# Attention and mixture of experts on one core: two requests change places, and one head's values stand later in the order

## The chip, the cores and the metric

The kernel runs on one core of a Trainium2 chip. The core has five engines with a queue of instructions each: TensorE (PE, matrix products; the loads of its stationary operand are shown as PEld), VectorE (DVE), ScalarE (ACT), GpSimd (POOL) and SyncE (SP). Each queue runs in order, and a queue waits for another through semaphores. Transfers between the main memory (HBM) and the on-chip memory (SBUF) run on DMA engines of their own, after GpSimd or SyncE has issued a request. Products are written to eight PSUM banks, from which ScalarE and VectorE read them.

The metric is the device time of one execution in microseconds (us), lower is better. The kernel before has a median of 375.86 us in three runs (375.83 to 376.34).

## The reference

Two stages. First attention over 4 batches, 8 heads, 768 positions and head width 64. Heads 0, 2 and 6 are retrieval heads: they see every earlier position. The other five are streaming heads: they see 4 sink positions and a window of 64. Then a mixture of 4 experts is computed for all 3072 tokens of width 512, with a hidden width of 1024; every expert runs on every token, weighted by its normalised probability.

```python
scores = scale * np.matmul(q, k.transpose(0, 1, 3, 2))
...
scores = np.where(mask[None, :, :, :], scores, -1000000000.0)
scores = scores - np.max(scores, axis=-1, keepdims=True)
a = np.exp(scores)
a = a / (np.sum(a, axis=-1, keepdims=True) + 1e-09)
return np.matmul(a, v).astype(np.float32)
...
p = domain_probs / (domain_probs.sum(-1, keepdims=True) + 1e-09)
for e in range(E):
    h = np.maximum(x @ w1[e], 0.0)
    out += p[:, e:e + 1] * (h @ w2[e])
```

Inputs and output are float32; the kernel computes its products in 16 bits.

## The kernel before

**Groups.** Attention is done in eight groups: batch b and half c of its positions (384 each), numbered g = 2b + c. Group 0 runs alone at the start. From then on the experts' products run on PE, and the steps of the next attention group are woven between them: `moe_steps` yields after each small piece of expert work, and a plan says how much attention should be done by then. Group 1 (batch 0, second half) is woven into the first part of the expert work, which takes three tiles of 128 tokens through one expert after the other (`plain_steps`): layer 1 (L1148, products with `w1sb`, followed by a Relu on ScalarE, L1161), then layer 2 (L1169, products with `w2sb`, added up by VectorE, L1181 and L1185). The order on every engine is the order in which this program calls the instructions.

**Requests.** Weights, and the inputs of group 1, are requested from GpSimd's queue in one list written by hand (lines 562 to 588). `landed(x)` is a tiny copy on GpSimd that waits until x has arrived, so that the list does not run too far ahead. `load_triples` (L230) brings k and q of group 1, `load_v` brings values (L304 for retrieval heads, into `vR`; L310 for streaming heads, into `vS`), `load_w1` (L327) and `load_w2` (L349, L354) bring an expert's weights. `load_w1` makes two requests, one for each half of the partitions; `load_v(0, 1, RH)` makes three, one for each retrieval head. In the built program a request also waits until the eighth request before it has landed.

**One attention group.** `attention(b, c)` first transposes k and q (for group 1 with products on PE, L622, copied to `qT`, `kR` and `kS` by VectorE at L637, L645 and L661; `kR` holds the keys of retrieval heads, `kS` those of streaming heads). Then it goes through the heads in `order`; group 1's is 0, 2, 1, 3, 6, 5, 7, 4. `scores(h)` makes one or more score tiles: products into a bank of `pA` (L736), the exponential on ScalarE into one of eight `es` buffers (L754), the mask on VectorE (L761 or L765). A retrieval head of group 1 has four tiles, a streaming head two. `values(h)` multiplies them with the values: L799 for retrieval heads (15 products of 65 columns in group 1, in several steps, with the normalisation at L824 to L828 and a transposing DMA on SyncE at L833 behind them), L863 for streaming heads (scaled by ScalarE's L878 and L881 and VectorE's L884).

A head's values come later than its scores. The loop holds the heads whose values are due in `waiting` and takes the first one out when two are waiting, or when one is waiting and the score tiles of the waiting heads and the new one are more than six. `both` then alternates steps of the new head's scores with steps of those values:

```python
ahead = sum(len(score_tiles(x)) for x in (*waiting, h))
if len(waiting) > 1 or (waiting and ahead > 6):
    done = waiting.pop(0)
    v_steps = values(done)
for m, step in enumerate(both(scores(h), v_steps)):
```

For groups 0 and 1 (`by_dma` false) the transposes of k and q stand between the heads; those of heads 6 and 7 (`transposes(3)`) come inside head 2's scores.

Of the kernel before, what the change touches and what calls it, by code (L numbers as in the profile page):

```python
# [19 lines left out]
def kernel(  # L20
# [36 lines left out]
    E, DM, F = moe_w1.shape  # L57
# [110 lines left out]
    def half(u):  # L168
        return slice(u * D, (u + 1) * D)
# [5 lines left out]
    def own_v(h):  # L175
        return half(PLACE[h][1])
# [10 lines left out]
    def v_tiles(b, c, h):  # L187

        if RETR[h]:
            return vR[b % 2][:, 3 * c : 3 * c + 3, RH.index(h), :]  # L190
        if b:
            return windows(vSf)[:, :, SH.index(h), :]
        return vS[:, c, :, SH.index(h), :]
# [10 lines left out]
    def rows_of(x, b, h, c):  # L204
        return x[b, h, c * CH : (c + 1) * CH, :].rearrange("(j p) d -> p j d", p=P)

    def tiles_of(x, b, h, c):
        return x[b, h, c * CH : (c + 1) * CH, :].rearrange("(t r) d -> r t d", r=TK)

    def windows_of(x, b, h, c):  # L210

        assert b > 0
        first = ((b * H + h) * S + c * CH - WO) * D
        return bass.AP(x.tensor, x.offset + first, [[D, P], [WQ * D, WT], [1, D]])
# [13 lines left out]
    def load_triples(x, dst, b, c, h0, h1):  # L228

        gp.dma_start(  # L230
            out=dst[:, h0:h1, :, :].rearrange("p h j d -> p h (j d)"),
            in_=x[b, h0:h1, c * CH : (c + 1) * CH, :].rearrange(
                "h (p j) d -> p h (j d)", j=3
            ),
        )
# [64 lines left out]
    def load_v(b, c, heads):  # L300
        for h in heads:
            t = v_tiles(b, c, h)
            if RETR[h]:
                gp.dma_start(out=t[:, :, 0:D], in_=rows_of(v, b, h, c))  # L304
            elif b:
                gp.dma_start(  # L306
                    out=t[:, :, own_v(h)], in_=windows_of(v, b, h, c)
                )
            else:
                gp.dma_start(  # L310
                    out=t[R0:P, :, own_v(h)],
                    in_=tiles_of(v, b, h, c),
                )
# [10 lines left out]
    def load_w1(e, f0, f1):  # L324
        x = moe_w1[e].rearrange("(u c d) f -> u d c f", u=2, c=DMP)
        for u in range(2):
            gp.dma_start(  # L327
                out=w1sb[half(u), e * DMP : (e + 1) * DMP, f0:f1],
                in_=x[u, :, :, f0:f1],
            )  # L330
# [219 lines left out]
    def landed(x):  # L550

        gp.tensor_copy(out=seen, in_=x)
# [5 lines left out]
    def w2_of(e):  # L558
        return w2sb[0:1, e * FTP, 0:1]
# [17 lines left out]
    landed(qt16[0:1, 0, 0, 0:1])  # L577
    load_triples(k, k16, 0, 1, HP, H)
    load_triples(q, qt16, 0, 1, HP, H)
    load_v(0, 1, RH)  # L580
    load_w1(2, 0, F)
    landed(w2_of(1))
    load_v(0, 1, SH[:2])
    load_w2(2)
# [15 lines left out]
    def attention(b, c):  # L600
# [238 lines left out]
        def x_transposes(h):  # L839
            ct = PLACE[h][0]  # L840
            x = x_pair if ct else x_one
            r = slice(0, P) if ct else half(0)
            ps = pV.tile([P, 512], FP32, name="pV", bufs=2)
            for j in range(3):
                nc.tensor.matmul(
                    out=ps[r, j * P : (j + 1) * P], lhsT=x[:, j, r], rhs=ident16,
                    start=True, stop=True,
                )
            nc.vector.tensor_copy(out=xT[g][r, ct, :], in_=ps[r, 0:CH])

        def values(h):
            if RETR[h]:
                yield from values_r(h)
                return
            ct, u = PLACE[h]
            ps = pV.tile([P, 512], FP32, name="pV", bufs=2)
            work = []
            for es, parts in es_of[h]:
                for t, o, q0, nq in parts:
                    work.append((es, t, o, q0, nq))  # L860
            ns = 0
            for n, (es, t, o, q0, nq) in enumerate(work):
                nc.tensor.matmul(  # L863
                    out=ps[:, q0 : q0 + nq],
                    lhsT=v_tile(b, c, h, t),
                    rhs=es[:, o : o + nq],
                    start=(n == 0),
                    stop=(n == len(work) - 1),
                    skip_group_check=True,
                )  # L870
                ns += mm_ns(nq)
                if ns > 300 and n < len(work) - 1:
                    yield ns
                    ns = 0

            r, o = half(u), half(1 - u)
            rc = att.tile([P, CH], FP32, name="rc", bufs=2)
            nc.scalar.activation(  # L878
                out=rc[r, :], in_=ps[o, 0:CH], func=AF.Ln, bias=eps[o, :]
            )  # L880
            nc.scalar.activation(out=rc[r, :], in_=rc[r, :], func=AF.Exp, scale=-1.0)  # L881

            def scale(r=r, ps=ps):
                nc.vector.tensor_tensor(  # L884
                    out=xT[g][r, ct, :], in0=ps[r, 0:CH], in1=rc[r, :], op=ALU.mult
                )

            later(scale, g)

            yield ns + (600.0 if g == 1 else 400.0)  # L890
# [36 lines left out]
        def both(a, bb):  # L927

            gens = [a, bb]
            while gens:  # L930
                for gg in list(gens):
                    try:
                        yield next(gg)
                    except StopIteration:
                        gens.remove(gg)

        by_dma = b > 0
        if not by_dma:
            alloc_qT(b, c)
        if first:  # L940
            yield from transposes(0)
            yield from scores(0)
            yield from scores(1)
            yield from transposes(2)
            yield from values(0)
            yield from scores(4)
            yield from scores(5)
            x_transposes(0)
            yield from transposes(1)
            yield from values_pair(1, 5)  # L950
            yield from scores(3)
            yield from transposes(3)
            yield from scores(2)
            yield from values(4)
            yield from both(scores(6), values(2))
            yield from scores(7)
            yield from values(6)
            yield from values_pair(3, 7)
            x_transposes(6)
            tick(LAG)  # L960
            small_things()
        else:
            order = (0, 2, 6, 1, 3, 5, 7, 4) if by_dma else (0, 2, 1, 3, 6, 5, 7, 4)
            more = divmod(g + 1, NCH) if g + 1 < G else None
            if not by_dma:
                sink_rows(b, c)

            def behind_values(h):
                if more and not RETR[h]:
                    load_v(*more, [h])  # L970
            if by_dma:
                keys_to_rows(b, c)
                yield 1500.0
            else:
                yield from transposes(0)
                yield from transposes(1)

            waiting = []
            for n, h in enumerate(order):
                v_steps, done = iter(()), None  # L980
                ahead = sum(len(score_tiles(x)) for x in (*waiting, h))
                if len(waiting) > 1 or (waiting and ahead > 6):
                    done = waiting.pop(0)
                    v_steps = values(done)
                for m, step in enumerate(both(scores(h), v_steps)):
                    yield step
                    if not by_dma and n == 1 and m == 1:
                        yield from transposes(3)
                if done is not None:
                    behind_values(done)  # L990
                waiting.append(h)
                if n < 3 and by_dma:
                    keys_to_windows(b, c, n)
                if n == 1 and by_dma:
                    sink_rows(b, c)
                if n == 3 and more and g > 1:
                    transpose_rows(*more)
                if not by_dma and n == 2:
                    yield from transposes(2)
            if more:  # L1000
                if g == 1:
                    load_probs(pair0)
                    transpose_rows(*more)
            for h in waiting:
                yield from values(h)
                behind_values(h)
# [39 lines left out]
    def tick(ns):  # L1046
        clock[0] += ns
        while behind and behind[0][0] <= clock[0]:
            behind.pop(0)[1]()
# [561 lines left out]
    for ns in attention(0, 0):  # L1611
        tick(ns)
# [108 lines left out]
```

## Time and profile before

| | |
|---|---|
| median of three runs | 375.86 us (375.83 to 376.34) |
| the profiled execution's own time | 376.48 us |
| its span, first to last instruction | 374.8 us |
| granted TensorE clock | 0.999 |
| GpSimd's requests in the stretch: L304 x3, L327 x2 | 34.37 to 36.59, 36.59 to 37.85 |
| first matmul of the third expert's layer 1 | 46.92 |
| `landed` on GpSimd behind those weights | 46.91, after 4.06 us of waiting |

The table of line groups shows what the expert work and the attention cost on each engine, with columns: line, engine, operation, output and inputs, shape, count, busy time, mean of one in ns, idle time before them and what ended it.

```profile
L1148 PE MATMUL pA<-xT,w1sb 128*128 128x384 f16 (+1 forms) x256 | 30.4, 272 | 1.9 <-DMA w1sb<-in_moe_w_dram 1.8
L1169 PE MATMUL pO<-w2sb,hA 128*128 128x512 f16 x128 | 30.6, 379 | 0.0
L736 PE MATMUL pA<-qT,kR 128*128 128x128 f16 (+2 forms) x141 | 23.1, 261 | 0.7 <-DVE kR L645 0.7
```

Busy time of PE is modelled up to the end of a matmul, while the next one already streams; the distance from start to start is the better measure of what one costs.

### The profile page before, as it was taken

Reading aid. Unit: us, or ns where it says so; the run is one execution under the profiler, and the core shown is the slowest. Engines: PE = TensorE matmul, PEld = TensorE weight load, DVE = VectorE, ACT = ScalarE, POOL = GpSimd, SP = SyncE. Lnnn points to the kernel's source line nnn. Section 1 sums busy time; section 2 is a strip of 40 time slices with the busy share of each in tenths; the row PEclk is TensorE's granted clock in tenths of the full one; section 3 lists DMA queues with packets and bytes.
Section 4 is the critical chain, followed back from the end, with each engine's and each line's share of the span. In section 5 each row is a group of like instructions: output and inputs, shape, how many; then the busy total and the mean of one; then the engine's idle time right before and its main releaser. Section 6 shows DMA issues by size and latency. Waiting matters only on the chain.

```text
span 374.8 us, 10310 instructions
## 1 busy us (share of the span) xinstructions
PE 365.4 (98%) x4219; PEld 310.5 (83%) x4219; DVE 277.9 (74%) x583; ACT 226.3 (60%) x471; POOL 113.0 (30%) x162
## 2 busy tenths in 40 slices
PE   7899899999999999999999999999999999999996
PEld 4655466678998988999989899988899998998995
DVE  4765867797787669868657858857768868979881
ACT  5644569547786785775776855784777361451630
POOL 8845573692057039015501650320000000000000
PEclk9999999999999999999999999999999999999999
DMA  9999999999799399988905990951220300300101
GB/s 181 190 208 207 196 172 191 182 205 106 111 104 160 83 98 129 158 109 76 189 3 65 172 153 13 140 121 12 72 68 2 108 10 2 114 3 14 44 3 58
DMA packets 122340, 39.65 MB, mean 106 GB/s; under 512 B 112192, under 2 KB 114820, under 8 KB 122292
## 3 DMA queue, kind: packets, MB, share of 16 engines
q0 software_dynamic: 82816, 19.01, 57.1%
q1 hardware_dynamic: 37876, 19.58, 23.5%
q8 instruction: 33, 0.54, 0.6%
q10 hardware_dynamic: 1600, 0.39, 0.5%
q14 instruction: 15, 0.12, 0.1%
HBM read 44.89 MB, written 6.34 MB: 137 GB/s over the span
## 4 chain that ended last, share of the span: by engine, by line
PE 85%; DMA 8%; POOL 4%; DVE 1%; issue 1%; ACT 0%; POOLq 0%
PE pO L1462 31%; PE pA L1282 22%; PE pO L1311 9%; DMA w1sb<-in_moe_w_dram 5%; PE pA L1148 5%; PE pA L736 5%; PE pO L1169 5%; DMA q<-in_q_dram 3%; PE pV L1311 2%; PE pA L1311 2%; PE pV L863 2%; PE pV L799 2%; DVE xs L1233 1%; POOL vR L304 1%; PE pA L1554 0%
## 5 line engine op out<-in xcount | busy, mean ns | idle before, releaser
L1462 PEld LDWEIGHTS <-hA 128*128 128x128 f16 x1104 | 104.8, 98 | 11.9
L1282 PE MATMUL pA<-xs,w1sb 128*128 128x256 f16 x768 | 97.2, 272 | 0.0
L1282 PEld LDWEIGHTS <-w1sb 128*128 128x128 f16 x768 | 71.8, 98 | 7.3
L1462 PE MATMUL pO<-w2sb,hA 128*128 128x256 f16 x640 | 76.8, 272 | 0.0
L754 ACT ACTIVATE es<-pA 128x384 f16<-128x384 f32 (+2 forms) x122 | 58.9, 511 | 27.5 <-PE pA L736 22.9
L1291 ACT ACTIVATE hA<-pA 128x512 f16<-128x512 f32 x96 | 57.2, 598 | 29.1 <-PE pA L1282 26.8
L306 POOL DMA_DIRECT2D vS<-in_v_dram x30 | 29.6, 988 | 113.2 <-PE pV L863 109.9
L1462 PE MATMUL pO<-tsb,hA 128*128 128x256 f16 x464 | 56.8, 272 | 0.0
L1233 DVE TENSOR_TENSOR xs<-xT,pB 128x1024 f16<-128x1024 f16 (+1 forms) x49 | 47.0, 976 | 2.7 <-DMA xT<-x_pair 2.7
L1067 DVE TENSOR_TENSOR hA<-hA 128x1024 f16<-128x1024 f16 x60 | 39.4, 684 | 0.6 <-PE pO L1462 0.3
L1161 ACT ACTIVATE hA<-pA 128x384 f16<-128x384 f32 (+1 forms) x64 | 22.2, 385 | 20.4 <-PE pA L1148 20.4
L1311 PEld LDWEIGHTS <-w1sb 128*128 128x128 f16 x512 | 31.3, 98 | 1.6 <-issue 0.5
L1148 PE MATMUL pA<-xT,w1sb 128*128 128x384 f16 (+1 forms) x256 | 30.4, 272 | 1.9 <-DMA w1sb<-in_moe_w_dram 1.8
L1169 PE MATMUL pO<-w2sb,hA 128*128 128x512 f16 x128 | 30.6, 379 | 0.0
L1148 PEld LDWEIGHTS <-w1sb 128*128 128x128 f16 x256 | 19.5, 98 | 10.9 <-issue 2.5
L1482 ACT COPY s<-pO 128x256 f32<-128x256 f32 x31 | 11.5, 372 | 27.3 <-PE pO L1462 21.8
L765 DVE TENSOR_TENSOR es<-es,mS 128x384 f16<-128x384 f16 (+1 forms) x40 | 13.8, 344 | 17.9 <-ACT es L754 17.9
L884 DVE TENSOR_TENSOR xT<-pV,rc 64x384 f16<-64x384 f32 x36 | 20.0, 555 | 8.3 <-ACT rc L881 7.7
L1328 DVE CUSTOM_DVE_ANT_0 hA<-pO,s 128x512 f16<-128x512 f32 x26 | 17.7, 688 | 9.9 <-PE pO L1311 8.5
L878 ACT ACTIVATE rc<-pV,eps 64x384 f32<-64x384 f32 x36 | 20.7, 576 | 6.6 <-PE pV L863 6.0
L1321 ACT COPY s<-pO 128x512 f32<-128x512 f32 x39 | 22.7, 587 | 3.2 <-PE pO L1311 3.0
L736 PE MATMUL pA<-qT,kR 128*128 128x128 f16 (+2 forms) x141 | 23.1, 261 | 0.7 <-DVE kR L645 0.7
(175 smaller groups left out, 519.1 us busy)
## 6 DMA issues: line engine op xcount, KB each, us to landing
pB<-p_rows SPq DMA_DIRECT2D x10, 512.0 KB
out_dram<-o SPq DMA_DIRECT2D x19, 256.0 KB
w1sb<-in_moe_w_dram POOLq DMA_DIRECT2D x8, 512.0 KB, 9.2
w2sb<-in_moe_w_dram POOLq DMA_DIRECT2D x4, 1024.0 KB, 12.1
vS<-in_v_dram POOLq DMA_DIRECT2D x30, 112.0 KB, 4.4
k_rows<-in_k_dram POOLq DMA_DIRECT2D x18, 128.0 KB, 5.3
q<-in_q_dram POOLq DMA_DIRECT2D x18, 128.0 KB, 6.2
out_dram<-hA SPq DMA_DIRECT2D x4, 256.0 KB
```

The source lines that it names most:

```text
L306: gp.dma_start(out=t[:, :, own_v(h)], in_=windows_of(v, b, h, c))
L736: nc.tensor.matmul(out=ps[:, o : o + nq], lhsT=key_tile(b, c, h, t), rhs=qTs[b, c][:, hp, q0 : q0 + nq], start=(n == 0 or not first), stop ...
L754: nc.scalar.activation(out=es[:, 0:cols], in_=ps[:, 0:cols], func=AF.Exp, scale=SC)
L1067: nc.vector.tensor_tensor(out=out, in0=a, in1=b, op=ALU.subtract)
L1148: nc.tensor.matmul(out=pss[ft][:, 0:cols_n], lhsT=w1_tile(e, ct, ft), rhs=x[:, ct, :], start=(n == 0), stop=(n == DMP - 1),)
L1169: nc.tensor.matmul(out=ps_o, lhsT=hs[:, ft, j * P : (j + 1) * P], rhs=w2sb[:, e * FTP + ft, :], start=(ft == 0), stop=(ft == FTP - 1),)
L1233: nc.vector.tensor_tensor(out=o, in0=xin, in1=pb.to_broadcast([P, DMP, n, P]), op=ALU.mult)
L1282: nc.tensor.matmul(out=ps[:, f * PC : (f + 1) * PC], lhsT=w1_tile(e, ct, f0 + f), rhs=xs[:, ct, :], start=(ct == 0), stop=(ct == DMP - 1),)
L1291: nc.scalar.activation(out=blocks[:, b0 : b0 + 2, k0 : k0 + 2, :].rearrange("p t f x -> p f t x"), in_=ps.rearrange("p (f t x) -> p f t x" ...
L1311: nc.tensor.matmul(out=ps[:, f * P : (f + 1) * P], lhsT=w_tile(e, w[:, ct, :], f), rhs=a[:, ct, :], start=(first and f == 0 and ct == 0), ...
L1321: nc.scalar.copy(out=kept[n], in_=ps)
L1462: nc.tensor.matmul(out=ps, lhsT=a[:, k, :], rhs=b(k), start=(first and k == 0), stop=(k == KT - 1), skip_group_check=not first,)
```

## The change

Two edits. In the list of requests, the three requests of group 1's retrieval values go behind the two of the third expert's first weights. In `attention`, the bound of six score tiles becomes eight for the groups 0 and 1, of which only group 1 uses this loop. In group 1 heads 0 and 2 have eight tiles together, which is more than six and not more than eight; so head 0's values are no longer taken out at head 2 but at the next head, 1, when two heads are waiting.

```diff
     load_triples(q, qt16, 0, 1, HP, H)
+    load_w1(2, 0, F)
     load_v(0, 1, RH)
-    load_w1(2, 0, F)
     landed(w2_of(1))
...
                 ahead = sum(len(score_tiles(x)) for x in (*waiting, h))
-                if len(waiting) > 1 or (waiting and ahead > 6):
+                if len(waiting) > 1 or (waiting and ahead > (6 if by_dma else 8)):
                     done = waiting.pop(0)
```

In the built program the same instructions stand on every engine in both versions. On PE, head 2's four score tiles come without head 0's values between them; the first seven of head 0's 15 values products then follow head 1's first score tile and precede the third expert's first layer-1 products, and the other eight stand around that expert's next tile. On VectorE the normalisation of head 0 (L824 to L828) goes behind the two masks of head 1. On GpSimd only the two requests change places. From the transposes of heads 4 and 5 (`transposes(2)`) on nothing is moved.

## The prediction

> **What bounds the kernel now.** The page's busy table comes first: TensorE (PE) is busy 98% of the span, so a change can only win where PE stands still, and only loses where it makes PE stand still.
>
> ```profile
> span 374.8 us, 10310 instructions
> PE 365.4 (98%) x4219; PEld 310.5 (83%) x4219; DVE 277.9 (74%) x583; ACT 226.3 (60%) x471; POOL 113.0 (30%) x162
> ```
>
> Next the chain of waits between 34 and 50 us, where the diff acts. Columns: start, length, what held the end.
>
> ```profile
> 34.37 2.22 POOL vR L304 x3
> 36.59 0.62 POOL w1sb L327
> 37.21 9.58 DMA w1sb<-in_moe_w_dram
> 46.79 0.14 issue
> 46.92 0.81 PE pA L1148 x4
> ```
>
> The third expert's first weights (two requests, L327) stand behind three requests of group 1's retrieval values (L304) on GpSimd, and the second half lands at 46.79. The reader is to see that PE starts that expert (L1148) only then. After 46.92 this chain holds PE work almost alone up to 110 us, so what PE gains or loses here reaches the end. Third, PE's timeline before that start:
>
> ```profile
> 41.66 0.27 PE L799 MATMUL pV<-vR,es 128*128 128x65 f16 x3 [0.18 <-ACT es L754]
> 45.59 0.33 PE L736 MATMUL pA<-qT,kR 128*128 128x384 f16 x1
> 46.92 0.81 PE L1148 MATMUL pA<-xT,w1sb 128*128 128x384 f16 x4 [1.01 <-DMA w1sb<-in_moe_w_dram]
> ```
>
> Two stops: one for an exponential, one of 1.01 us for the weights. The listed busy time hides part of them, since ends of matmuls are modelled; by starts, a 384-column matmul takes 0.163 (24 of L1148 from 49.14 to 53.05), so PE was free at 45.59 + 0.17 = 45.76 and stood 1.16. At 41.19 four L799 matmuls began, which take 0.12 at 0.03 each (seven from 45.13 to 45.34); the next began at 41.66, another 0.35. Together 1.5 us, the most that this place can give. Fourth, VectorE's timeline, which decides my forecast:
>
> ```profile
> 42.51 0.36 DVE L761 TENSOR_TENSOR es<-es,mC 128x384 f16<-128x384 f16 x1 [1.68 <-ACT es L754]
> 42.78 0.68 DVE L1067 TENSOR_TENSOR tsb<-w2sb,tsb 128x1024 f16<-128x1024 f16 x1
> 43.38 0.74 DVE L1185 SCALAR_TENSOR_TENSOR hA<-pO,p_sb,hA 128x512 f32<-128x512 f32 x1
> 44.05 0.79 DVE L637 CAST qT<-pA 128x384 f16<-128x384 f32 x1
> 44.68 0.80 DVE L645 CAST kR<-pA 64x384 f16<-64x384 f32 x1
> 45.49 0.81 DVE L661 CAST kS<-pA 64x384 f16<-64x384 f32 x1
> ```
>
> From 42.51 these six run without a gap, and the last, which writes head 7's keys into kS, ends at 45.49 + 0.81 = 46.30.
>
> **Part one, the requests.** Nothing is added: three L304 requests (0.74 each, 2.23) and two L327 (0.62 each, 1.26) change places. The weights are requested at 34.37 instead of 36.59, the values at 35.63 instead of 34.37. What this does to landing is read from the DMA view of single issues (last column: us from issue to landing):
>
> ```profile
> q<-in_q_dram POOLq DMA_DIRECT2D x1, 192.0 KB, 6.0
> vR<-in_v_dram POOLq DMA_DIRECT2D x1, 48.0 KB, 5.7
> w1sb<-in_moe_w_dram POOLq DMA_DIRECT2D x1, 512.0 KB, 7.3
> ```
>
> The request ahead of all five, q at 33.63, lands at 39.63; the third vR (35.8) at 41.5; the first half of w1 (36.59) at 43.9, the second at 46.79. They land in the order of issue, one behind the other, with the DMA engines busy throughout. So the values occupy 41.5 − 39.63 = 1.9 us, and without them in front the weights land at about 44.9. The bounds: no gain, if they were only interleaved (46.79), and 2.2, the whole shift of the issue (44.6). I take 1.9. The first vR took 0.85 behind q (34.37 + 6.1 = 40.5), hence lands at about 45.75.
>
> What GpSimd issues behind them keeps its order. In the built program each request waits for the landing of the eighth before it, so the last three vS requests (40.84 to 42.85) now wait for the two halves of w1 and the first vR, up to 45.8. They stand behind the third expert's w2 in the queue, which lands at 52.45 (39.95 + 12.5) either way, and head 5, their first user, comes past 60. The fourth expert's w1 (47.38) goes out some 0.5 earlier at best, behind the same transfers; it landed at 60.0 for a use at 61.52. This costs nothing; if that cover were gone, L1148 at 61.52 would be late next.
>
> **Part two, the order on PE.** The test `ahead > 6` becomes 8 for group 1 only. Head 0's values (15 L799 matmuls in group 1) no longer run between head 2's scores but between those of head 1. The same instructions remain, 15 matmuls of about 0.03 each moved past the first L1148. PE after the change, from 41.19 (start of what follows head 2's first scores, the same in both): two 256-column scores 0.22 (44.05 to 44.27 before), four L1169 0.86 (44.27 to 45.13), twelve L622 0.45 (42.72 to 43.17), four L1169 0.86, two scores 0.22 (45.34 to 45.56), four L1169 0.86, one 0.17: 44.83. None of these meets a wait; the exponentials whose banks they take end by 43.0.
>
> Now comes head 1's first score tile, ahead of head 0's values and L1148. **Its second weight load waits in the built order for the L661 copy that ends at 46.30.** Before, the same wait stood behind L1148 (47.57), where it cost nothing. That copy doesn't move: it is the end of the gapless row that starts when ScalarE has done head 2's first exponential (42.48), which stays fifth in ScalarE's order; the exponential that is newly early comes behind it. So the wait on weights turns into a wait on VectorE, from 44.83 to 46.30. Then: release 0.08 (an estimate between the 0.02 and 0.14 that "issue" takes in the chain), two score matmuls 0.11 (three take 47.57 to 47.74), seven L799 0.21: L1148 starts at 46.70 instead of 46.92, with weights (44.9) and vR (45.75) there. What is left to do differs: eight L799 more (0.25), one score tile less (0.17). Net 0.22 − 0.08 = **0.14 us gained** of the 1.5.
>
> ScalarE's exponential for head 1 takes a buffer that head 0's fourth values matmul frees (46.8 on); the Relu of L1148 behind it is ready at 47.5, so nothing is held. VectorE's normalisation of head 0 (L824 to L828, 0.15 + 0.18 + 0.36) slides behind head 1's masks, as does SP's transposing DMA (48.50, then about 49.5); its result is next touched by L884 at 57.55. The PSUM bank of L637 (49.61 + 0.80 before) is free for the third hidden tile of those 24 L1148 at about 50.3 against a need at 50.3; a hundredth or two may be lost.
>
> **Sum.** 376.48 (the profiled run's own time, 374.8 of it span, 1.7 around it) − 0.14 = 376.34. The median shown is 0.62 lower, 375.86; the same step gives **375.7**.
>
> **Rivals.** (1) *The copy does not hold PE.* If VectorE is through earlier than this execution shows, vR's landing decides: values at 45.75, L1148 at 45.96, gain 0.96 − 0.08 = 0.88: 375.0. For it: part one truly clears the weights. Against: the wait is in the built order and the six VectorE rows have no gap to lose.
>
> (2) *Slower: the copy pins PE where the weights did not.* The profiled run is 0.62 longer than the median; if the DMA wait is part of that, PE waits less for w1 in ordinary runs, while the copy holds the new order all the same. Without any wait the old order starts L1148 at 45.76, the new one at 46.70 with 0.08 more to do: 1.02 lost, 376.9. It decides as soon as w1 lands before some 46.65 in the old order, and passes 0.75 lost at about 45.9. Against: L661 itself hangs on earlier PE work, and q and k loads came through the same queue.
>
> (3) *The values come late.* vR now stands behind 1 MB of weights, and PE's in-order queue holds L1148 behind the values. The two vS requests that followed w1 before landed 8.8 and 8.5 us after issue (46.9, 47.3); at 47.3 L1148 starts at 47.5 and 0.7 is lost: 376.5. It decides from a landing past 46.5. Against: the bytes in front are the same as those that had landed by 46.79. Issues of 0.62 for w1 at 36.59, during L637 and L645 (36.78 to 38.2), are as long as all others (617 to 637 ns), so GpSimd does not look locked out. The Trainium skill (SBUF — State Buffer, "SBUF: two separate sides") warns of that lockout: VectorE in a two-port mode keeps GpSimd from writing descriptors. By that rule vR, now issued during the same copies, would be what suffers; the row speaks against it.
>
> (4) *The weights land no sooner.* w1 still at 46.79: L1148 at 46.92, 0.08 lost, 375.9; within the forecast's own range.
>
> **Chances.** Forecast with (4) 0.56; (1) 0.24; (2) 0.13; (3) 0.07. A difference under 0.2% (0.75 us) is about what a measurement of this kernel can tell from no change. (1) ends faster in nearly all its share, 0.23 in total. (2) and (3) pass 0.75 in the greater part: slower 0.16. The rest, 0.61, is within. The range reaches to (1) and to most of (2): 374.9 to 376.7; the forecast's own is 375.4 to 376.1.
>
> **What would show it.** Right: no wait on w1sb at the first L1148 of that expert, a PE stop of about 1.5 us charged to VectorE at the kS scores (L736) ending near 46.4, vR landing after w1 by 46. Wrong: a stop charged to vR, L661 ending before 45.5, or a w1 wait that stays; and a difference past 0.75 either way.

## The result: slower by a quarter of a per cent

The changed kernel has a median of 376.93 us (14 runs, 375.89 to 378.59), the kernel before on the same chip 375.98 (14 runs, 375.58 to 377.24). The ratio is 1.0025, with an interval of 1.0013 to 1.0037. Two later series of the same program gave 1.0015 (1.0007 to 1.0024) and 1.0019 (1.0006 to 1.0032). So the loss is real, 0.6 to 0.95 us by the medians of the three, where 0.14 us of gain had been forecast; 376.93 also lies above the range, which ended at 376.7.

The first trace of the changed kernel (time 376.67 us, the one of before had 376.48) does not look like a failed forecast. From the page of its profile, the same lines as before:

```profile
span 374.9 us, 10308 instructions
...
PE 364.9 (97%) x4219; PEld 310.2 (83%) x4219; DVE 278.1 (74%) x583; ACT 226.5 (60%) x471; POOL 113.7 (30%) x162
...
L1148 PE MATMUL pA<-xT,w1sb 128*128 128x384 f16 (+1 forms) x256 | 30.4, 273 | 1.3 <-DMA w1sb<-in_moe_w_dram 1.2
```

The idle time of L1148 for `w1sb` fell from 1.8 to 1.2 us, and all that is left of it belongs to the first expert, at 20.8 us. In PE's timeline the third expert no longer waits for weights:

```profile
45.12 0.26 PE L736 MATMUL pA<-qT,kS 128*128 128x64 f16 x2
46.52 0.24 PE L736 MATMUL pA<-qT,kS 128*128 128x160 f16 x1 [1.14 <-DVE kS L661]
46.60 0.38 PE L799 MATMUL pV<-vR,es 128*128 128x65 f16 x7
46.82 0.81 PE L1148 MATMUL pA<-xT,w1sb 128*128 128x384 f16 x4
```

The wait stands where it had been foreseen, at head 1's scores, on VectorE's copy into `kS`. The chain of waits (start, length, what held the end) shows what is behind it: VectorE's row without a gap, from the moment ScalarE had done head 2's first exponential.

```profile
41.19 1.48 ACT es L754 x3
...
42.69 0.36 DVE es L761
43.05 0.60 DVE tsb L1067
43.65 0.66 DVE hA L1185
44.31 0.71 DVE qT L637
45.02 0.63 DVE kR L645
...
45.66 0.81 DVE kS L661
46.48 0.05 issue
46.52 0.24 PE pA L736
```

The requests did what they should. The two halves of the third expert's first weights were issued at 34.55 and 35.17 and landed at 42.06 and 44.68, the three values right behind them, at 44.89, 45.21 and 45.54. The DMA view of the issues from 33.5 to 36.5 us, whose last column is the time from issue to landing (the median of both halves in the first line, the first value in the second):

```profile
w1sb<-in_moe_w_dram POOLq DMA_DIRECT2D x2, 512.0 KB, 8.5
...
vR<-in_v_dram POOLq DMA_DIRECT2D x1, 48.0 KB, 9.1
```

From the first expert's first product (20.79; before 20.55) to the run of 24 products of the third (49.02; before 49.14) this execution took 28.23 us, against 28.59 before. By this pair of traces the change wins 0.36 us in its stretch, and loses 0.27 near 247 us, where PE waits for VectorE and that for a transposing DMA (x_pair, L833). Neither explains a loss of 0.6 to 0.95.

### The profile page after: what moved, and what is told of

Its sections match the earlier page's. It is cut to its first block, busy times and chain, and to the rows that moved or that the text cites. A ratio compares the mean times of both kernels' runs of the same rounds, so it can differ in the third digit from the quotient of the medians.

```text
span 374.9 us, 10308 instructions
## 1 busy us (share of the span) xinstructions
PE 364.9 (97%) x4219; PEld 310.2 (83%) x4219; DVE 278.1 (74%) x583; ACT 226.5 (60%) x471; POOL 113.7 (30%) x162
## 3 DMA queue, kind: packets, MB, share of 16 engines
HBM read 44.89 MB, written 6.34 MB: 137 GB/s over the span
## 4 chain that ended last, share of the span: by engine, by line
PE 85%; DVE 6%; DMA 5%; POOL 1%; issue 1%; ACT 1%; POOLq 0%; DVEq 0%
PE pO L1462 29%; PE pA L1282 21%; PE pO L1311 9%; PE pA L1148 7%; PE pO L1169 7%; PE pA L736 4%; DMA w1sb<-in_moe_w_dram 2%; PE pV L1311 2%; PE pA L1311 2%; PE pV L799 2%; DVE xs L1233 2%; PE pV L863 2%; DMA xT<-x_pair 1%; DMA hA<-in_v_dram 1%; DVE hA L1067 1%
## 5 line engine op out<-in xcount | busy, mean ns | idle before, releaser
L1148 PE MATMUL pA<-xT,w1sb 128*128 128x384 f16 (+1 forms) x256 | 30.4, 273 | 1.3 <-DMA w1sb<-in_moe_w_dram 1.2
L1148 PEld LDWEIGHTS <-w1sb 128*128 128x128 f16 x256 | 19.4, 98 | 10.1 <-issue 1.7
```

Of the source, the lines that this page charges most:

```text
L1148: nc.tensor.matmul(out=pss[ft][:, 0:cols_n], lhsT=w1_tile(e, ct, ft), rhs=x[:, ct, :], start=(n == 0), stop=(n == DMP - 1),)
```

## The experiments

Four explanations were tried. P: the steps are right and the rest is chance. C: a long stop of PE lets the clock fall in part of the executions. D: a transfer is late elsewhere, through the new order of the requests. R, the second rival of the prediction: in ordinary executions of before the weights come sooner than in the one trace of it, so that the copy holds PE where the weights did not. S is the opposite of R: the long wait of the first trace is the usual one. All ratios are to the kernel before in the same series.

**The changed program again (e1, e9, and single traced executions e15, e17, e18).** Only a comment was added.

> The changed kernel once more, nothing edited. Theory P (the step as predicted, the rest is chance between executions): ratio to the kernel before between 0.998 and 1.001. Theory C (the new long stop of PE, 1.1 to 1.4 us on the key copy, makes the clock gate drop in part of the executions): ratio 1.002 to 1.004, and where an execution is long its granted clock is near 0.995. Theory D (a transfer moved by the new order of requests is late in part of the executions): ratio 1.002 to 1.004 at a clock of 1.000.

> The changed kernel with a comment added. Two things decide: its ratio, and what TensorE waits for. Theory R (the copy holds TensorE until 46.5 us in every execution of the changed kernel, where in before the weights let it go at 45.9 in some executions and at 46.9 in others): the stop on kS L661 of 1.0 to 1.2 us is there again, first product of the third expert near 46.8, ratio 1.001 to 1.0025. Theory D (a transposing transfer near 245 us comes late in the changed kernel more often): a wait of 0.2 us or more at the product near 247 us.

> The changed kernel, one more look. Theory R: TensorE stands for 1.0 to 1.2 us on VectorE's copy into kS, as in all three traces of it, however early the weights land; theory S the same. They differ in before alone; this look counts the two kernels evenly.

> The changed kernel, a look to count with. Theory R: the stop on VectorE's copy into kS again 1.0 to 1.2 us, the 24th product of the third expert starting 0.1 to 0.4 us sooner after the first expert's first product than in the first trace of before (where it took 28.6 us); the other looks at before have 0.3 to 0.8 us sooner. What is lost apart from that (start at 20 us, product at 247 us) lies between -0.5 and 0.5 us.

> A second look of the same kind. Theory R: a stop of 1.0 to 1.2 us on VectorE's copy into kS, and the 24th product of the third expert 0.1 to 0.4 us sooner after the first expert's first product than in the first trace of before.

Measured: e1 376.65 us (11 runs), e9 376.72 (11 runs), with the ratios given above; the single executions took 375.96, 376.00 and 376.50. The stop on `kS` was 1.1 us in each of these traces. P falls, since three series agree on a loss.

**The kernel before again (e5, and single traced executions e6, e13, e14).** Here, too, only a comment was added.

> The program of before with a comment added. Its median should be the one of before (ratio 1.000, interval within 0.15% either way); any larger difference is what two builds of one program show here. Its trace: theory S (the stop of 1.5 us for the third expert's weights in the first trace is usual) expects TensorE to wait 1.0 to 1.3 us for w1sb(2) again, with w1(2) landing 26.0 to 26.5 us after the first expert's first product. Theory R (the second rival of the prediction: in ordinary executions the weights come sooner than in the trace of before, so that the copy pins TensorE where the weights did not) expects a wait of 0.8 us or less. Theory C (the stop at 20 us for the first expert's weights can be followed by a stretch at half the clock) expects none here if that stop is under 1 us.

> Before again, one look. The same three expectations as for the other look at before: S a wait of 1.0 to 1.3 us for w1sb(2), R 0.8 us or less; C a full clock from the first stretch on. The time should lie in 375.4 to 377.5.

> Before, one more look at how long TensorE waits for w1sb(2). Theory R: the landing of these weights wanders by a microsecond between executions of before (46.79, 46.77 and 45.76 us in three), and the wait with it (1.0, 0.8 and none); a fourth should again lie between none and 1.1, and the stretch from the first expert's first product to 49 us be shorter the shorter the wait is. Theory S: 1.0 or more, 45.76 was an exception.

> The same question as the look before it: theory R a wait between none and 1.1 us, theory S 1.0 us or more.

Measured: e5 376.13 us (12 runs; ratio 0.999, 0.9969 to 1.001); the single executions 376.27, 375.99 and 375.99. What matters is PE's timeline of e5 around the third expert's start:

```profile
45.65 0.33 PE L736 MATMUL pA<-qT,kR 128*128 128x384 f16 x1
45.90 0.81 PE L1148 MATMUL pA<-xT,w1sb 128*128 128x384 f16 x4
...
48.11 1.46 PE L1148 MATMUL pA<-xT,w1sb 128*128 128x384 f16 x8
49.77 1.46 PE L1148 MATMUL pA<-xT,w1sb 128*128 128x384 f16 x8 [0.20 <-DVE qT L637]
```

The expert starts at 45.90 instead of 46.92, and no wait for weights is listed, since they had landed at 45.76. At 49.77 a small wait appears that the first trace did not have: VectorE's copy of queries (L637), which frees a PSUM bank. Of the 1.02 us that came free, this takes back 0.35. All traces of the two kernels together (times in us; "PE at 60" and "at the end" compare the start of the same matmul with the first trace of before; + is later):

| execution | weights landed | first expert's first L1148 | run of 24 L1148 | PE at 60 | at the end | time |
|---|---|---|---|---|---|---|
| before, first | 46.79 | 20.55 | 49.14 | 0 | 0 | 376.48 |
| before, e5 | 45.76 | 20.67 | 48.11 | -0.68 | -0.71 | 375.77 |
| before, e6 | 46.77 | 20.80 | 49.12 | -0.02 | -0.21 | 376.27 |
| before, e13 | 46.00 | 20.74 | 48.35 | -0.61 | -0.52 | 375.99 |
| before, e14 | 46.20 | 20.26 | 48.55 | -0.60 | -0.49 | 375.99 |
| changed, first | 44.68 | 20.79 | 49.02 | -0.12 | +0.15 | 376.67 |
| changed, e1 | 45.14 | 20.85 | 49.30 | +0.16 | -0.04 | 376.45 |
| changed, e9 | 44.63 | 20.60 | 48.84 | -0.31 | -0.13 | 376.38 |
| changed, e15 | 45.45 | 20.45 | 48.81 | -0.34 | -0.53 | 375.96 |
| changed, e17 | 44.81 | 20.58 | 48.81 | -0.33 | -0.52 | 376.00 |
| changed, e18 | 44.83 | 20.62 | 48.86 | -0.28 | -0.01 | 376.50 |

In before the landing wanders by a microsecond and PE's start with it; the first trace had the latest landing of the five. Counted from start to start, as the prediction counted its 1.16 us, PE stood 1.16, 0.08, 0.95, 0.23 and 0.91 us for these weights, in the order of the table. (In e14 they landed early, but the whole execution ran 0.3 us ahead.) In the changed kernel the weights land 0.8 us apart and it makes no difference, because the copy sets the start: from the first expert's first product to the run of 24 it takes 28.23 to 28.45 us, the kernel before 27.44 to 28.59, the less the shorter that stop.

The means at 60 us are -0.38 for before and -0.20 for the changed kernel, so on average it is 0.18 us behind there, and 0.21 at the end. S falls: the first trace had the longest stop, and two of five have next to none. The means have the sign that R expects, but executions of before alone differ by 0.7, so that with five and six traces the standard error of the 0.18 is about 0.17; the sign is not settled by them. The times of these profiled executions differ in the mean by 0.23 (376.10 and 376.33), the medians of the timed series by 0.6 to 0.95.

**Only the requests (e2).** Before, with the weights requested ahead of the values, and PE's order as it was:

```diff
-    load_v(0, 1, RH)
     load_w1(2, 0, F)
+    load_v(0, 1, RH)
```

> Only the requests change places; head 0's values stay between head 2's scores. All theories expect PE to stop at the first L799 of head 0 from about 41.3 until the first vR lands, 44.9 in the changed kernel's trace: 3.6 us, against 1.5 us of stops that go. Ratio 1.005 to 1.007 by the sum. If the clock gate reacts to a long stop (theory C), 3.4 us or more of half clock come on top: 1.009 and more, and clocks near 0.995. Theory D expects long executions here at full clock, as the requests are those of the changed kernel.

Measured: 381.15 us (4 runs), ratio 1.014 (1.0122 to 1.0157), far above the 1.005 to 1.007 of the sum. PE's list of waits from 15 to 60 us (total, times, longest):

```profile
PE pV L799 <- DMA vR<-in_v_dram: 3.0, 1, 3.0
PE pA L1148 <- DMA w1sb<-in_moe_w_dram: 2.1, 1, 2.1
```

Head 0's values, in their old place, wait 3.0 us for `vR`. So the first edit needs the second and can't be priced by itself. The rest of the 5 us is, in this trace, the second line (the first expert's weights, 0.8 before) and a stretch at half the clock from 21.2 us on, both ahead of the place where the edit acts. The other three runs have a mean clock of 0.990 to 0.995 too; whether the stop at 46.7 has a part in that is not shown.

**Only the order (e3).** Before, with the bound of eight tiles:

```diff
-                if len(waiting) > 1 or (waiting and ahead > 6):
+                if len(waiting) > 1 or (waiting and ahead > (6 if by_dma else 8)):
```

> Only head 0's values move behind head 2's scores; the requests stay as before, so the weights land near 46.8 and vR near 41. PE stops once, from 44.8 to 46.9. By the sum L1148 starts where it did before with 0.08 us more to do: ratio 1.000 (theory P). Theory C: this stop is the longest of all orders but that of the requests alone, so 1.002 to 1.005, with clocks near 0.995 in the long executions. Theory D: the requests are those of before, so 0.999 to 1.001 and no long executions beyond those of the kernel before.

Measured: 377.00 us (12 runs), ratio 1.0018 (1.0003 to 1.0034). The copy holds PE for 1.1 us here too. The traced execution is one of the two longest (378.56 us), with half the clock from 21.2 to 24.6; the section on the chip shows it. Without its two runs at a mean clock of 0.995 the median is 376.62. Theory P had expected a ratio of 1.000. The order alone is thus enough for a loss like that of both edits (1.0015 in the same series). Whether the earlier weights are worth anything beside it is left open by this run, since the two ratios can't be told apart.

**The copy sooner (e4) and later (e10).** The changed kernel, with head 7's keys copied ahead of head 6's, and with that copy made twice:

```diff
-                for u in range(2):
+                for u in (1, 0) if hp == 3 and not first else (0, 1):
```

```diff
-                    nc.vector.tensor_copy(out=x_out, in_=x_in)
+                    for _ in range(2 if hp == 3 and not first else 1): nc.vector.tensor_copy(out=x_out, in_=x_in)
```

> The changed kernel, and in the transposes of heads 6 and 7 head 7's key copy (L661) runs before head 6's (L645). The stop of PE ends with L661, now at about 45.5 instead of 46.3, 0.8 us sooner. The step of the prediction: L1148 at 46.0, a gain of 0.14 + 0.8 = 0.9 us on the kernel before, ratio 0.9975 (theory P). Theory C: the stop shrinks to 0.3 to 0.7 us and the clock holds: 0.9975 too, with clocks of 1.000. Theory D: the requests are those of the changed kernel, so long executions at full clock remain: ratio 0.999 to 1.001.

> The changed kernel with head 7's copy into kS made twice in group 1 (the second writes the same), so that VectorE lets TensorE go one copy, 0.8 us, later. Theory R, and the prediction's step that the copy is what holds TensorE: the stop grows from 1.1 to 1.9 us and the kernel by 0.7 to 0.8 us: ratio of before 1.003 to 1.0045. If the copy did not set the end, nothing is added: ratio 1.001 to 1.0025. Theory C (a stop of nearly 2 us makes half-clock stretches likelier): some runs at a mean clock of 0.995 with 2 us more.

Measured: e4 376.24 us (12 runs), ratio 0.9999 (0.999 to 1.0009); e10 376.97 us (6 runs), ratio 1.0044 (1.0018 to 1.007), where the changed kernel in the same series had 1.0019. PE's waits of e4 (from 40 to 250 us), then of e10 (from 40 to 60):

```profile
PE pO L1311 <- ACT hA L1291: 0.7, 1, 0.7
PE pA L736 <- DVE kS L661: 0.5, 1, 0.5
```

```profile
PE pA L736 <- DVE kS L661: 2.0, 1, 2.0
```

The stop is 0.5, 1.1 and 2.0 us with the copy 0.8 sooner, in its place, and one copy (0.80) later. PE at 60 us stands at -0.27, -0.20 (the mean of six) and +0.64. The lower end is flatter, partly because this execution of e4 began the first expert late (20.86). So the copy sets the end of this stretch: doubled, it adds 0.84 us there. In the timed runs the ratio of e4 is 0.0016 under that of the changed kernel in the same series, which is 0.6 us, as much as its stop lost; P and C had expected 0.9975, and the number that D had named fits as well. Of e10 the timed runs say less: the median of e10 is 0.25 above that of e9, and its ratio rests in part on one execution of 380.44 at a mean clock of 0.995. The interval is wide enough to hold both the 0.7 to 0.8 expected and no addition at all; it is the trace that decides here. The first line of e4 is the place near 247 us, where that execution lost 0.65.

**No wait in either order (e7, e8).** e7 is before, with the third expert's first weights in halves, so that its first products need half of them; e8 is the changed kernel, with head 7's keys copied by ScalarE, and first (with e4's edit):

```diff
-    load_w1(2, 0, F)
+    load_w1(2, 0, F // 2); load_w1(2, F // 2, F)
```

```diff
-                    nc.vector.tensor_copy(out=x_out, in_=x_in)
+                    (nc.scalar.copy if hp == 3 and not first else nc.vector.tensor_copy)(out=x_out, in_=x_in)
```

> Before, with the third expert's first weights requested as two halves of the columns in the place where they stand, and nothing else: the first products of that expert need the first half alone, which by the trace of before would land near 44 us instead of 46.8. No copy is moved ahead of them, so nothing takes the wait's place but vR's half microsecond at most. Theory S: the 1.16 us of that wait go and nothing comes instead: 375.0 against 376.1, ratio 0.997 (0.996 to 0.998). Theory R: the wait is shorter in ordinary executions, so 0.3 to 0.5 us: ratio 0.9985 to 0.9995. A theory by which the time saved here is eaten by a later wait (the transposing transfer near 245 us): no change, ratio 1.000, with TensorE waiting 0.5 us or more there.

> The changed kernel, but head 7's keys are copied by ScalarE and first, so that TensorE no longer waits for VectorE's copy near 46 us; in the changed kernel that stop is 1.1 us. The prediction's steps (the whole stop of 1.5 us goes when neither copy nor weights hold TensorE, up to vR's landing at 44.9 to 45.9): 374.9 to 375.3, ratio 0.997 to 0.998 of before and 1.3 to 2 us under the changed kernel. Theory R: the same gain against the changed kernel in the step, but from an ordinary before whose stop is shorter: ratio 0.998 to 0.9995. Theory D (the new order of requests costs elsewhere, whatever TensorE does at 46 us): ratio 0.999 to 1.001.

Measured: e7 376.39 us (12 runs), ratio 1.0005 (0.9986 to 1.0025): no gain, where S and R had both expected one; nor does its trace list the wait near 245 us that the third theory named. e8 375.66 us (12 runs), ratio 0.9983 (0.9964 to 1.0002). In e7 the wait for the first weights is gone, the expert starts at 46.05, and by 48.26 PE is 0.88 us ahead of the first trace of before. Then two things take it back: L637 holds PE for 0.28 at 50.0, and the chain of waits shows the second weights:

```profile
41.57 11.67 DMA w2sb<-in_moe_w_dram
53.24 0.04 issue
53.28 1.02 PE pO L1169 x4
```

At 60 us only 0.16 of the 0.88 is left. Without its wait on the first weights, this version is held by VectorE and then by the second weights. The last is in part the edit's own: the second weights were requested at 41.57, behind two requests more, 1.6 us later than in the first trace of before. In e8 both the copy and its share of VectorE's row are away from PE; PE stands at -1.46 at the run of 24, and after a wait for the second weights at -0.88 at 60 us. What is left of waits from 40 us on:

```profile
PE pO L1311 <- DVE xs L1067: 0.5, 1, 0.5
PE pO L1169 <- DMA w2sb<-in_moe_w_dram: 0.4, 1, 0.4
PE pO L1311 <- ACT hA L1361: 0.2, 1, 0.2
```

**The place near 247 us (e11, e12).** e11 is the changed kernel, with the row transposes of the next group issued one head later, so that the transposing DMA of x_pair goes ahead of six others on SyncE. e12 is e8 with that, and with the second weights requested ahead of two values:

```diff
-                if n == 3 and more and g > 1:
+                if n == 4 and more and g > 1:
```

> The changed kernel with the row transposes of the next group's keys and queries issued one head later (n == 4 in place of n == 3), so that the transposing transfer of x_pair goes ahead of six others on SyncE's queue, in every group behind the second. If theory D holds, the wait near 247 us goes (0.3 us in the trace of the changed kernel, none in the one of its second submission) and with it most of what the change costs: ratio 0.9995 to 1.001. Theory R: 0 to 0.3 us less than the changed kernel: ratio 1.0005 to 1.002.

> A candidate to beat both kernels: the changed kernel with head 7's keys copied by ScalarE and first, the transposing transfer of x_pair ahead of the six others, and the third expert's second weights requested before the values of heads 1 and 3. With the first edit alone the trace had 0.4 us of wait for w2sb at 52.5 and 0.5 us at 247 us left; both should go. Expected 0.6 to 0.9 us under that one: ratio of before 0.996 to 0.998.

Measured: e11 379.63 us (6 runs), ratio 1.0105 (1.0085 to 1.0126); e12 378.30 us (5 runs), ratio 1.006 (1.0048 to 1.0072). Both miss by far. PE's waits of e11 from 60 us on:

```profile
PE pA L736 <- DMA qT<-q: 2.3, 2, 1.5
PE pO L1311 <- DVE xs L1067: 0.5, 1, 0.5
```

The six transposes have no slack themselves: one head later, scores wait for `qT` in two places, 1.5 and 0.8 us, and the wait near 247 stays; in e12 it is 0.8 us, and two waits for `qT` cost 0.9. In the 20 traces PE waits between nothing and 0.8 us at that place, as a rule longer where the first transposing issue of `kT` on SyncE is longer (1.85 to 2.64 us in the 18 traces without the edit of e11). The rule is loose: an issue of 2.36 comes with a wait of 0.3 us in the first trace of the changed kernel, and with none in e10. D finds no support in the traces of the changed kernel, since from 246 us to the end they lose -0.19 to +0.28 against the first trace of before, and the other traces of before -0.18 to +0.11; the means are 0.03 and 0.00.

**The version that is faster (e16).** e8, and the third expert's second weights requested ahead of the values of heads 1 and 3:

```diff
-    load_v(0, 1, SH[:2])
     load_w2(2)
+    load_v(0, 1, SH[:2])
```

> The version in which ScalarE copies head 7's keys first, with the third expert's second weights requested ahead of the values of heads 1 and 3 too; SyncE's order stays as it was. With the copy alone: 0.4 us of wait for w2sb at 52.5 us, 375.66 us against 376.31. If that wait goes and nothing comes: 0.3 to 0.4 us less, ratio of before 0.9965 to 0.998. If the next wait takes its place: 0.998 to 0.999.

Measured: 375.30 us (10 runs, 374.63 to 376.03) against 376.13; ratio 0.9978 (0.9966 to 0.9989). Between 40 and 60 us the trace lists no wait of PE, and PE at 60 us stands at -1.65. The chain of waits in that stretch is PE's own work; the rows around the third expert's start:

```profile
45.10 0.35 PE pV L799 x7
45.45 0.65 PE pA L1148 x4
...
47.56 4.01 PE pA L1148 x24
...
51.94 0.86 PE pO L1169 x4
```

It keeps both edits of the change. In its trace VectorE's copy has left PE's way: 0.8 us of VectorE's gapless row went to ScalarE. What each part is worth is not shown: e8 has the copy's move alone, and its interval just reaches 1; the earlier second weights were not measured without it.

## Why the prediction was wrong

Part one was right: 1.9 us of earlier landing had been worked out, 44.9; measured 44.68. The values came at 44.89, sooner than the 45.75 forecast; nothing waited for them. Rival 3 did not occur, and neither did rival 4.

Part two was right in kind and place. The stop on L661 ended at 46.52 (forecast: copy at 46.30 and release 0.08) after 1.14 us by the list (1.5 from start to start had been forecast; two short score products ran ahead of it). The first L1148 came at 46.82, forecast 46.70, in an execution that had begun the first expert 0.24 later. The gain against the trace of before in this stretch was 0.36 us there and 0.30 on average over six executions (28.59 less 28.23, 28.45, 28.24, 28.36, 28.23 and 28.24), where 0.14 had been forecast.

The step that failed is the last one of the sum: "The median shown is 0.62 lower, 375.86; the same step gives 375.7." A gain worked out against one execution's wait was carried over to executions whose wait is shorter. The trace of before had the latest landing of five, 46.79; the others had 46.77, 46.20, 46.00 and 45.76. Its stop of 1.16 us, which the forecast let the change remove, was 0.9 us in two of them and 0.08 and 0.23 in the other two. The copy's wait is there in all six traces of the changed kernel, 1.14 to 1.15 us. So in place of 0.14 gained the traces show 0.30 gained against the first execution and 0.2 lost against the mean of five; the timed series show 0.6 to 0.95 lost.

That is rival 2, which had been given 0.13. Its condition, weights landing before some 46.65, held in three executions of five, but clearly only in e5 and e13: in e14 PE was there 0.3 us sooner as well, and still stood 0.91 us. Its price was too high: at a landing near 45.9 it named 0.75 lost, and the execution with 45.76 was at 60 us 0.48 ahead of the changed kernel's mean (-0.68 against -0.20). It had left out that the old order meets VectorE too, a little later: L637 took back 0.35 in that execution. The prediction knew this bank and priced it at "a hundredth or two", for the new order alone. That the 376.9 of this rival is the median that was measured is chance, as far as the traces go.

The first rival named 0.88 us of gain if the copy does not hold PE. In e8 it does not, and PE at 60 us stood just 0.88 ahead; but that is luck. The rival let `vR`'s landing at 45.75 set the start at 45.96. In e8 `vR` landed at 44.98 and L1148 began at 45.46, in an execution that began the first expert 0.20 later; the run of 24 stood 1.46 us ahead, and the wait for the second weights, which the rival does not have, took back 0.44 of it. The median was 0.65 under that of before.

The size of the loss is not shown. The traces of the changed kernel are 0.2 us behind those of before on average, with a spread of some 0.7 among executions of one kernel; its timed runs are 0.6 to 0.95 behind. Half-clock stretches do not make up the difference: without the three runs at a mean clock of 0.995 the changed kernel's median over all its series is 376.63 (36 runs), and that of before, likewise, 376.04 (103 runs whose clock is on record). No trace caught one of the many changed-kernel runs between 376.7 and 377.8. The trace of e4 (376.87) is a hint that such a run may lose 0.65 near 247 us, but nothing shows why the change should make that commoner. So it is shown that the copy sets PE's start in the changed kernel, and that in two of five executions of before the weights let PE go clearly sooner. The timed runs point to the same stop: the order alone brings the loss (e3), and a stop shorter by 0.6 us takes it away (e4). But the traces put the step at 0.2 us, which their spread can't tell from nothing; what makes up the rest of the loss is open.

## What to carry to other kernels

Before a wait on a transfer is priced, look at it in several executions: here its end wandered by 1.0 us, the one trace at hand had its worst case, and a gain against it, 0.14 by forecast and 0.30 as measured, was 0.2 us of loss against the mean of five. A variable wait is not worth exchanging for a fixed one that ends near the latest end of the variable one. Where PE's waits move from one engine to the next as each is removed (weights, copy, bank, second weights), count the work of the engine that runs without a gap, and move some of it to one with room: with that, and with the second weights requested sooner, the same reordering went from a loss of 0.25% to a gain of 0.22%.

## What the chip showed beside it

In the trace of the order alone (e3) PE waits 1.73 us for the first expert's weights, up to 21.16 us, and then runs at half its clock. The table by stretches (window, length, busy time of PE, PEld, DVE, ACT and POOL with counts, granted clock, DMA share, GB/s):

```profile
18.00:21.20 3.20, 1.47 (x28) 1.00 (x25) 2.27 (x9) 1.50 (x4) 1.97 (x5) 1.00 1.11 207
21.20:24.60 3.40, 3.40 (x11) 1.53 (x12) 3.19 (x13) 0.00 (x0) 1.51 (x3) 0.50 1.12 211
24.60:28.00 3.40, 3.31 (x21) 1.90 (x20) 1.05 (x4) 2.67 (x7) 0.93 (x2) 1.00 1.12 210
```

The clock is 0.50 for 3.41 us, although PE is busy all through; 11 matmuls fall into that window, 21 into the next one of the same length. By half of that time it costs some 1.7 us, an estimate. The trace of e2 has the same 3.41 us, from 21.22 on, at the end of a stop of 2.10 us. The other 18 traces, with a wait of 0.3 to 1.5 us in that place, kept the full clock. Both traces have a mean clock of 0.995; so have three of 39 runs of the changed kernel and three of 106 of before.

The Trainium skill (TensorE: Matmul & The Clock Gate, "Why this matters for your kernels") advises against gaps of more than about 3 us between bursts of matmuls. These two traces have the fall with stops of 1.73 and 2.10 us, so a stop well under that bound is not safe here. Its length does not decide alone: the stop of 2.96 us at 46.7 in e2's trace and the one of 1.98 in e10's kept the full clock, the first with PE busy for 0.44 us of 3.40 (43.4 to 46.8). What decides between these places is open.

In all 20 traces the requests of GpSimd's queue landed in the order in which they were issued, even a 48 KB one 0.2 us behind 1 MB in front of it (44.68 and 44.89): here the place in the list, not the size, decided when a small transfer was there.
